# Attention scores computed transposed on halves of the TensorE array's columns, and the read-out's factors multiplied in at its eviction

## The chip, the cores and the metric

The kernel runs on one core of a Trainium2 chip. The metric is device time in microseconds (us); a run's time is that of one execution of the whole program. PE is TensorE, DVE VectorE, ACT ScalarE, POOL GpSimd and SP SyncE, which here only issues transfers.

## The reference

For 8 batches with 8 heads, 512 tokens of width 64 (`x`) and 32 states per head (`state`):

```python
scores = scale * x @ state.T                  # per head: 512 tokens x 32 states
a = softmax(scores, axis=-1)                  # over the 32 states
xread = a @ state                             # 512 x 64
scores2 = scale * state @ x.T                 # the same numbers, transposed: 32 x 512
a2 = softmax(scores2, axis=-1)                # over the 512 tokens
sread = a2 @ x                                # 32 x 64, "the read-out"
rows = concat([xread, sread], axis=2)         # 4608 rows of 512 over all heads
h = rows @ w_in                               # MoE 1, 512 -> 1024
u = layernorm(h * softmax(h)) * g_ln
y = u @ w_out                                 # 1024 -> 512
out = relu(y @ w2_in)**2 @ w2_out             # MoE 2, 512 -> 2048 -> 512
```

Both softmaxes subtract the row's maximum and divide by the sum plus 1e-9.

## The kernel before

**Two phases.** Phase 1 (to about 485 us) does attention and MoE 1 batch by batch, phase 2 MoE 2. The heavy matrix products are done in three passes over operands split into two `fp32r` parts. The attention products between `x` and the states are plain `f32` products; the trace records each of them as two matmul records, and each transpose as one. `xread @ w_in` is folded into `a @ (state @ w_in)`: `emit_sw` makes `sw = state @ w_in` for a batch, `emit_l1` multiplies the transposed softmax `aT` with it.

**Attention of one batch.** Two heads make a pair `hp`, and four heads a group `g` (G = 2); `q` counts the two pairs of a group. `bdf` holds the states as block-diagonal columns with zeros beside them. `scores(b, tp)` (L359) makes scores for half of the tokens: tokens on partitions, the 256 head-state columns along the free axis. ACT copies them to `s_sb` (L367). `softmax_n` takes the softmax over states from `s_sb`: maximum on DVE (L379), subtraction on POOL or DVE (L248), exponential on ACT, sum and reciprocal on DVE (L390 to L392), product on POOL or DVE (L395), result `a_sb`. For the second softmax `emit_sT` (L406) transposes `s_sb` into PSUM (`sTp`), DVE takes the maximum over tokens there (L414), ACT the exponential with the sum as a by-product (L417, `eT`), DVE the reciprocal `l` (L429, L430), and ACT builds `dr`, the identity scaled by `l` (L433). `emit_e` (L447, tile `ep`) multiplies `eT` with `dr`, which transposes back and applies the factor in one f32 product; the copy overwrites `s_sb`. `sread` (L482, tile `srd`) multiplies `x_n` with it, and four small copies put the blocks on the diagonal into `xs`, the rows of the state part.

**The loop.** For batch `b` and `k` of 0 to 7: `emit_lnT` transposes a slice of the normed rows (`lnTp`, evicted to `lt`), `emit_l2` multiplies it with `wo[k]` (the `y` records), and between its four column groups `after[c]` sets pieces of the attention of batch `b+2` and `emit_l1` of batch `b+1`. Scores, `sTp`, `ep`, `aTp`, `srd` and `lnTp` share a pool of two PSUM banks (tag `m`).

**What sets the order.** A planner (`Flow`) runs while the program is built. PE's order is that of the code. Tasks of the other engines are queued with planned costs and due times, and the engine and the place of each instruction come from them: `fl.pe(cost, ...)` advances PE's planned time, a `yield {"V": 0.7}, f, ...` asks for DVE. Each engine then executes its list in that order. At the start SP loads the weights of MoE 1 as 8-byte words, and ACT, DVE and POOL decode them (`decode`: L287, L290, L293, L296, then the split at L242 and L248): eight chunks of `w_in` (`dec_e`, `dec_lt`) and eight of `w_out` (`dec`, then `wo`), which `emit_l2` of batch 0 needs one per `k`.

Of the kernel before, what the change touches and what calls it, by code (L numbers as in the profile page):

```python
# [148 lines left out]
def attn_solu_relu2_kernel(  # L149
# [193 lines left out]
    s_sb, a_sb, aT, sw, u_t, lt, yps, bds = {}, {}, {}, {}, {}, {}, {}, {}  # L343
# [4 lines left out]
    def scores(b, tp):  # L348

        if tp == 0:  # L350
            s_sb[b] = ap_.tile([P, T, HN], F32, tag="s", name="s_sb")
            a_sb[b] = ap_.tile([P, T, HN], F32, tag="a", name="a_sb")
# [16 lines left out]
        done["s", b, tp] = f  # L369
        done["a", b, tp] = fl.spawn(softmax_n(b, tp, f), 8.0 if b else 1.0)  # L370

    def softmax_n(b, tp, f):
        s = s_sb[b][:, 2 * tp:2 * tp + 2, :].rearrange("p t (h n) -> p (t h) n", n=NS)
        a = a_sb[b][:, 2 * tp:2 * tp + 2, :].rearrange("p t (h n) -> p (t h) n", n=NS)
        q = 2 * H
        yield None, 0.0, lambda: f["done"] is not None
        f = f["done"]
        mx = smp.tile([P, q, 1], F32, tag="mx", name="mx")
        f = yield {"V": 0.68}, f, lambda e: nc.vector.tensor_reduce(  # L379
            out=mx, in_=s, axis=AX.X, op=ALU.max  # L380
        )
# [12 lines left out]
        f = yield {"V": 1.2}, f, total
        f = yield {"P": 1.2, "V": 0.69}, f, lambda e: eng_of[e].tensor_tensor(  # L395
            out=a, in0=a, in1=sm.to_broadcast([P, q, NS]), op=ALU.mult
        )
        return f

    def emit_sT(b, g):  # L400


        ps = pm.tile([P, T, P], F32, tag="m", name="sTp")
        fl.pe(0.11 * T, pm_slot(), done["s", b, 0], done["s", b, 1])
        for t in range(T):
            nc.tensor.transpose(ps[:, t, :], s_sb[b][:, t, g * P:(g + 1) * P], ident)  # L406
        pf = ps.rearrange("p t q -> p (t q)")
        et = ap_.tile([P, S], F32, tag="eT", name="eT", bufs=1)
        dr = smp.tile([P, P], F32, tag="dr", name="dr", bufs=1)
        l = smp.tile([P, 1], F32, tag="l2", name="l2", bufs=1)  # L410
        nm = smp.tile([P, 1], F32, tag="m2", name="m2", bufs=1)

        def exps(f):
            f = yield {"V": 0.7}, f, lambda e: nc.vector.tensor_reduce(  # L414
                out=nm, in_=pf, axis=AX.X, op=ALU.max, negate=True
            )
# [5 lines left out]
        first = fl.spawn(exps(fl.end + 0.15), 1.0)  # L422
        pm_free.append(first)

        def rest():
            yield None, 0.0, lambda: first["done"] is not None

            def total(e):
                nc.vector.tensor_scalar(out=l, in0=l, scalar1=1e-9, scalar2=None, op0=ALU.add)  # L429
                nc.vector.reciprocal(out=l, in_=l)  # L430

            f = yield {"V": 0.35}, first["done"], total
            f = yield {"A": 0.4}, f, lambda e: nc.scalar.activation(  # L433
                out=dr, in_=ident, func=AF.Copy, scale=l
            )
            return f

        done["eT", b, g] = et, dr, fl.spawn(rest(), 3.0)

    def emit_e(b, g):  # L440


        et, dr, f = done.pop(("eT", b, g))
        ps = pm.tile([P, T, P], F32, tag="m", name="ep")
        fl.pe(0.23 * T, pm_slot(), f)
        for t in range(T):
            nc.tensor.matmul(  # L447
                out=ps[:, t, :], lhsT=et[:, t * P:(t + 1) * P], rhs=dr, start=True, stop=True
            )

        def gen(f):
            yield None, 0.0, lambda: all(("sub", b, tp) in done for tp in range(T // 2))
            f = yield {"A": 0.6, "V": 0.65}, f, copy(s_sb[b][:, :, g * P:(g + 1) * P], ps)
            return f

        done["e2", b, g] = fl.spawn(gen(fl.end + 0.15), 3.0)
        pm_free.append(done["e2", b, g])

    def emit_aT(b, g):
        f = fl.need([done["a", b, tp] for tp in range(T // 2)])  # L460
# [4 lines left out]
        for t in range(T):  # L465
            nc.tensor.transpose(ps[:, t, :], a_sb[b][:, t, g * P:(g + 1) * P], ident)
# [582 lines left out]
```

## Time and profile before

| | |
|---|---|
| median of 3 runs | 1250.4 us (1249.65 to 1250.83) |
| the profiled execution | 1249.4 us, its span 1247.6 us |
| mean granted clock of TensorE | 0.989 of 2.4 GHz |
| PE busy | 1199.0 us (96%) |
| DVE, ACT, POOL busy | 596.0, 523.8, 206.0 us |

The span runs from the first to the last instruction; 1.8 us of the execution's time lie outside it. A matmul's own duration contains the length of the pipeline, so the time that a run of matmuls takes is read from its start to the start of the next run.

### The profile page before, as it was taken

The numbers are of one execution on the slowest core, as the hardware profiler recorded it, in microseconds if no ns is written. First come the engines' busy times: TensorE is split into PE (matmuls) and PEld (weight loads), VectorE is DVE, ScalarE is ACT, GpSimd is POOL, SyncE is SP. The second block draws the span as 40 slices with busy tenths as digits, with TensorE's granted clock in tenths as the row PEclk, the third lists the DMA queues.
The fourth block names the chain that finished last, engine by engine and source line by source line (L and its number), as shares of the span: only waits on it lengthen the run. The fifth ranks groups of instructions, "written<-read, shape, count | busy, mean of one in ns | idle before, by whom it ended". The sixth has DMA issues, their size and how long they took to land.

```text
span 1247.6 us, 14707 instructions
## 1 busy us (share of the span) xinstructions
PE 1199.0 (96%) x5792; PEld 991.4 (79%) x5792; DVE 596.0 (48%) x940; ACT 523.8 (42%) x937; POOL 206.0 (17%) x243
## 2 busy tenths in 40 slices
PE   5679999999999999979999999999999999999998
PEld 3368888888888887757888888888888888888887
DVE  6975675763854559995322323223223223223232
ACT  4575775765855646544322223223223222222222
POOL 4553133132220423442000000000000000000000
PEclk8899999999999999989999999999999999999999
DMA  7322113112110126541201002002002002010000
GB/s 259 125 82 74 69 40 117 63 46 77 52 58 34 40 86 200 159 152 58 68 1 35 34 1 68 1 1 68 1 1 68 1 1 68 1 51 1 1 34 18
DMA packets 35429, 71.99 MB, mean 58 GB/s; under 512 B 3488, under 2 KB 20896, under 8 KB 34336
## 3 DMA queue, kind: packets, MB, share of 16 engines
q1 hardware_dynamic: 35360, 71.05, 17.2%
q8 instruction: 45, 0.74, 0.2%
q14 instruction: 24, 0.20, 0.1%
HBM read 53.22 MB, written 17.83 MB: 57 GB/s over the span
## 4 chain that ended last, share of the span: by engine, by line
PE 80%; DVE 9%; ACT 5%; DMA 3%; issue 2%; POOL 0%; SPq 0%; ACTq 0%; DVEq 0%
PE o L967 27%; PE h L952 26%; PE y L732 12%; PE hps L662 7%; PE sps L359 2%; PE srd L482 2%; PE lnTp L697 2%; DMA raw<-w_out 2%; DVE dec L290 2%; DVE dec L293 1%; DMA raw<-w_in 1%; ACT e L633 1%; DVE dec L296 1%; PE ep L447 1%; PE hps L513 1%
## 5 line engine op out<-in xcount | busy, mean ns | idle before, releaser
L967 PE MATMUL o<-wb,g 128*128 128x512 f32 x1632 | 398.1, 392 | 9.9 <-DVE g L248 5.4
L952 PE MATMUL h<-yt,wa 128*128 128x512 f32 (+1 forms) x1728 | 394.8, 378 | 0.0
L967 PEld LDWEIGHTS o<-wb,g 128*128 128x128 f32 x1632 | 305.8, 189 | 76.9 <-DVE g L248 8.5
L952 PEld LDWEIGHTS h<-yt,wa 128*128 128x128 f32 x1728 | 314.0, 188 | 61.5
L936 DVE TENSOR_TENSOR r<-r 128x512 f32<-128x512 f32 (+1 forms) x144 | 107.1, 744 | 370.3 <-ACT r L929 370.3
L929 ACT ACTIVATE r<-h 128x512 f32<-128x512 f32 (+1 forms) x144 | 82.5, 573 | 380.5 <-PE h L952 380.5
L732 PE MATMUL y<-lt,wo 128*128 128x512 f32 (+1 forms) x864 | 219.2, 394 | 2.4 <-DVE lt L706 2.0
L732 PEld LDWEIGHTS y<-lt,wo 128*128 128x128 f32 x864 | 150.0, 191 | 28.1 <-DVE lt L706 2.9
L248 DVE TENSOR_TENSOR g<-r,g 128x512 fp32r<-128x512 f32 (+1 forms) x144 | 97.3, 676 | 77.8 <-ACT g L242 71.4
L242 ACT CAST g<-r 128x512 fp32r<-128x512 f32 (+1 forms) x144 | 85.9, 597 | 99.8 <-DVE r L936 98.8
L248 POOL TENSOR_TENSOR yt<-yraw,yt 128x1024 fp32r<-128x1024 f32 (+1 forms) x9 | 20.6, 2288 | 531.6 <-ACT yt L242 531.6
L662 PE MATMUL hps<-sw,aT 128*128 128x512 f32 x368 | 98.2, 415 | 1.8 <-ACT sw L242 1.8
L662 PEld LDWEIGHTS hps<-sw,aT 128*128 128x128 f32 x368 | 69.5, 190 | 23.2 <-issue 6.3
L706 DVE SCALAR_TENSOR_TENSOR lt<-lnTp,g_sb,lt 128x512 fp32r<-128x512 f32 (+1 forms) x72 | 51.5, 716 | 53.9 <-ACT lt L703 53.6
L598 DVE TENSOR_REDUCE hm<-hps 128x1 f32<-128x512 f32 x68 | 46.4, 682 | 47.9 <-PE hps L662 45.8
L242 ACT COPY u<-hps 128x512 f32<-128x512 f32 x68 | 39.7, 584 | 51.5 <-DVE hm L598 49.5
L703 ACT ACTIVATE lt<-lnTp,g_sb 128x512 fp32r<-128x512 f32 (+1 forms) x72 | 48.2, 669 | 11.0 <-PE lnTp L697 10.6
L627 DVE SCALAR_TENSOR_TENSOR u<-u,e 128x1024 f32<-128x1024 f32 x34 | 42.1, 1240 | 13.6 <-ACT e L622 13.6
L633 ACT ACTIVATE e<-u,nmu 128x1024 f32<-128x1024 f32 x34 | 39.1, 1151 | 13.6 <-DVE nmu L630 13.0
L622 ACT ACTIVATE e<-u,nmx 128x1024 f32<-128x1024 f32 x34 | 39.1, 1150 | 12.2 <-issue 7.4
L248 DVE TENSOR_TENSOR sw<-hps,sw 64x512 fp32r<-64x512 f32 (+1 forms) x52 | 35.7, 688 | 14.1 <-ACT sw L242 13.7
L359 PE MATMUL sps<-bdf,xT 128*128 128x128 f32 x256 | 33.5, 288 | 9.2 <-DMA xT<-x_t 6.4
(97 smaller groups left out, 969.7 us busy)
## 6 DMA issues: line engine op xcount, KB each, us to landing
raw<-w_out SPq DMA_DIRECT2D x24, 512.0 KB, 3.5
out<-osb SPq DMA_DIRECT2D x34, 256.0 KB, 2.2
xT<-x_t SPq DMA_DIRECT2D x16, 512.0 KB, 5.3
xn<-x_n SPq DMA_DIRECT2D x8, 1024.0 KB, 4.9
y_d<-ys SPq DMA_DIRECT2D x16, 512.0 KB, 2.6
yraw<-y_d SPq DMA_DIRECT2D x16, 512.0 KB, 5.7
raw<-w_in SPq DMA_DIRECT2D x16, 512.0 KB, 3.8
raw_u<-w_in SPq DMA_DIRECT2D x8, 512.0 KB, 9.1
```

What stands on the lines that cost most here:

```text
L242: nc.scalar.copy(out=out, in_=in_)
L248: return lambda e: eng_of[e].tensor_tensor(out=out, in0=in0, in1=in1, op=ALU.subtract)
L359: nc.tensor.matmul(out=ps[:, j, g * P:(g + 1) * P], lhsT=xT[b][:, 2 * g + (q + b) % 2, (2 * tp + j) * P:(2 * tp + j + 1) * P], rhs=bdf[b][ ...
L633: f = yield {"A": 1.16}, f, lambda e: nc.scalar.activation(out=e_, in_=u, func=AF.Square, bias=nmu, accum_out=vs)
L662: nc.tensor.matmul(out=ps, lhsT=lhsT(i, k), rhs=rhs(j, k)[:, cs], start=(k == 0 and n == 0), stop=(k == n_k - 1 and n == len(passes) - 1),)
L703: f = yield {"A": 0.1 + nt * 0.143}, f, lambda e: nc.scalar.activation(out=o[:, 0], in_=pf, func=AF.Copy, scale=gk)
L706: f = yield {"V": 0.1 + nt * 0.155}, f, lambda e: nc.vector.scalar_tensor_tensor(out=o[:, 1], in0=pf, scalar=gk, in1=o[:, 0].bitcast(F32), ...
L732: nc.tensor.matmul(out=ps, lhsT=wo[k][:, w, c * P:(c + 1) * P], rhs=o[:, a], start=(k == 0 and i == 0), stop=(k == K1 - 1 and i == 2),)
L929: first = one({"A": 0.06 + n / 1000}, lambda e: nc.scalar.activation(out=r, in_=hps, func=AF.Relu))
L936: f = yield {"V": 0.15 + n / 960}, first["done"], lambda e: nc.vector.tensor_tensor(out=r, in0=r, in1=r, op=ALU.mult)
L952: nc.tensor.matmul(out=hps, lhsT=wa[m][:, w, k, :], rhs=yt[j][:, a, k, :], start=(k == 0 and i == 0), stop=(k == KD - 1 and i == 2),)
L967: nc.tensor.matmul(out=ops[j][t], lhsT=g[:, a, t * P:(t + 1) * P], rhs=wb[m][:, w, :], start=(m == 0 and i == 0), stop=(m == K2 - 1 and i ...
```

## The change

**Scores.** `scores(b, g)` now computes the scores of a group of four heads transposed: the states are the stationary operand with 64 columns (`bdf[..., 128 q : 128 q + 64]`), all 512 tokens move, and the product for `q` writes PSUM partitions 64 q to 64 q + 63, which is one half of the array's columns. `s_sb` holds head-states on partitions and tokens along the free axis. `xT` is loaded in halves by head pairs, not by tokens.

**Softmax over tokens.** `max_t` takes the maximum from `s_sb` in SBUF; `exp_t` lets ACT write `eT` with the sum `l2`. There is no `dr`: `emit_e` is four plain transposes. `sread` has 64 columns of `e` as stationary operand and the 128 columns of `x_n` moving, again by halves; its eviction (`sr`, two ACT instructions) multiplies by the reciprocal of `l2`, a factor per partition. `emit_xs` then transposes `sr` back (`xsp`), and the four copies to `xs` read that.

**Softmax over states.** `emit_sT` transposes `s_sb` to tokens on partitions; maximum and subtraction read PSUM, both on DVE; the rest is as before, per group `g`, not per half of the tokens.

**First batch's `sw`.** `emit_sw_first` is written by halves in the same way.

The core of the diff (new `scores`, `exp_t`, parts of `emit_sT`, `sread`, `emit_xs`, and the order):

```diff
-    def scores(b, tp):
...
-        ps = pm.tile([P, 2, HN], F32, tag="m", name="sps")
+    def scores(b, g):
...
+        ps = pm.tile([P, S], F32, tag="m", name="sps")
         slot = pm_slot()
-        for j in range(2):
-            fl.pe(0.87, slot, done["xT", b, tp])
-            for g in range(G):
-                for q in range(2):
-                    nc.tensor.matmul(
-                        out=ps[:, j, g * P:(g + 1) * P],
-                        lhsT=xT[b][:, 2 * g + (q + b) % 2, (2 * tp + j) * P:(2 * tp + j + 1) * P],
-                        rhs=bdf[b][:, g, 64 * q:64 * q + P],
-                        start=(q == 0),
-                        stop=(q == 1),
-                    )
-        s = s_sb[b][:, 2 * tp:2 * tp + 2, :]
+        for q in range(2):
+            fl.pe(0.6, slot, done["xT", b, g])
+            nc.tensor.matmul(
+                out=ps[64 * q:64 * q + 64, :],
+                lhsT=bdf[b][:, g, P * q:P * q + 64],
+                rhs=xT[b][:, 2 * g + (q + b) % 2, :],
+                start=True,
+                stop=True,
+            )
+        s = s_sb[b][:, g, :]
...
+        done["s", b, g] = f
+        done["nm", b, g] = fl.spawn(max_t(b, g, s, f), 6.0)
...
+    def max_t(b, g, s, first):
...
+        f = yield {"V": 0.65}, first["done"], lambda e: nc.vector.tensor_reduce(
+            out=nm, in_=s, axis=AX.X, op=ALU.max, negate=True
...
+        et = e_T[b, g] = ap_.tile([P, S], F32, tag="eT", name="eT", bufs=1)
...
+            yield None, 0.0, lambda: task["done"] is not None
+            f = yield {"A": 0.82}, task["done"], lambda e: nc.scalar.activation(
+                out=et, in_=s, func=AF.Exp, bias=nm, accum_out=l
+            )
...
+    def emit_sT(b, g):
...
+        if g == 0:
+            a_sb[b] = ap_.tile([P, G, T, P], F32, tag="a", name="a_sb")
+        ps = pm.tile([P, T, P], F32, tag="m", name="sTp")
+        fl.pe(0.11 * T, pm_slot(), done["s", b, g])
+        for t in range(T):
+            nc.tensor.transpose(ps[:, t, :], s_sb[b][:, g, t * P:(t + 1) * P], ident)
+        q = T * P // NS
...
+        def subs(f):
             f = yield {"V": 0.7}, f, lambda e: nc.vector.tensor_reduce(
-                out=nm, in_=pf, axis=AX.X, op=ALU.max, negate=True
-            )
-            f = yield {"A": 0.82}, f, lambda e: nc.scalar.activation(
-                out=et, in_=pf, func=AF.Exp, bias=nm, accum_out=l
-            )
+                out=mx, in_=pv, axis=AX.X, op=ALU.max
+            )
+            f = yield {"V": 0.7}, f - fl.HOP, sub(a, pv, mx.to_broadcast([P, q, NS]))
...
+            f = yield {"A": 0.62}, first["done"], lambda e: nc.scalar.activation(
+                out=a, in_=a, func=AF.Exp
...
     def emit_e(b, g):
-        et, dr, f = done.pop(("eT", b, g))
         ps = pm.tile([P, T, P], F32, tag="m", name="ep")
-        fl.pe(0.23 * T, pm_slot(), f)
+        fl.pe(0.11 * T, pm_slot(), done.pop(("eT", b, g)))
+        et = e_T.pop((b, g))
         for t in range(T):
-            nc.tensor.matmul(
-                out=ps[:, t, :], lhsT=et[:, t * P:(t + 1) * P], rhs=dr, start=True, stop=True
-            )
...
+            nc.tensor.transpose(ps[:, t, :], et[:, t * P:(t + 1) * P], ident)
...
     def sread(b):
-        ps = pm.tile([P, HP, P], F32, tag="m", name="srd")
-        e, xb = s_sb.pop(b), xn.pop(b)
...
+        ps = pm.tile([P, G, P], F32, tag="m", name="srd")
+        e, xb, l = s_sb.pop(b).rearrange("p g (t q) -> p g t q", q=P), xn.pop(b), l2[b]
...
-        for hp in range(HP):
-            g = hp // 2
-            fl.pe(0.22 * T, slot, done["xn", b], done["e2", b, g])
+        for g in range(G):
             for t in range(T):
-                nc.tensor.matmul(
-                    out=ps[:, hp, :],
-                    lhsT=xb[:, t, hp * P:(hp + 1) * P],
-                    rhs=e[:, t, g * P:(g + 1) * P],
-                    start=(t == 0),
-                    stop=(t == T - 1),
-                )
+                for q in range(2):
+                    hp = 2 * g + (q + b) % 2
+                    fl.pe(0.16, slot, done["xn", b], done["e2", b, g])
+                    nc.tensor.matmul(
+                        out=ps[64 * q:64 * q + 64, g, :],
+                        lhsT=e[:, g, t, 64 * q:64 * q + 64],
+                        rhs=xb[:, t, hp * P:(hp + 1) * P],
+                        start=(t == 0),
+                        stop=(t == T - 1),
+                    )
+        sr = ap_.tile([P, S], F32, tag="eT", name="sr", bufs=1)[:, :HN].rearrange(
+            "p (g q) -> p g q", g=G
+        )
...
+            f = yield {"V": 0.3}, f, total
+            def scaled(e):
+                for g in range(G):
+                    nc.scalar.activation(
+                        out=sr[:, g, :], in_=ps[:, g, :], func=AF.Copy, scale=l[:, g:g + 1]
...
+            f = yield {"A": 0.6}, f, scaled
...
+    def emit_xs(b):
+        sr, f = done.pop(("sr", b))
+        ps = pm.tile([P, G, P], F32, tag="m", name="xsp")
+        fl.pe(0.22, pm_slot(), f)
+        for g in range(G):
+            nc.tensor.transpose(ps[:, g, :], sr[:, g, :], ident)
...
-                    copy(
-                        xs[rows, hp:HP:2, b * NS:(b + 1) * NS], ps[rows, hp:HP:2, c0:c0 + NS]
-                    )(e)
+                    copy(xs[rows, hp:HP:2, b * NS:(b + 1) * NS], ps[rows, :, c0:c0 + NS])(e)
...
             for q in range(2):
-                fl.pe(0.87, ready, done["bdf", 0], done["w_f", 2 * g + q, c])
+                fl.pe(0.6, ready, done["bdf", 0], done["w_f", 2 * g + q, c])
                 nc.tensor.matmul(
-                    out=ps, lhsT=bdf[0][:, g, 64 * q:64 * q + P], rhs=w_f[2 * g + q, c],
-                    start=(q == 0), stop=(q == 1),
+                    out=ps[64 * q:64 * q + 64, :], lhsT=bdf[0][:, g, P * q:P * q + 64],
+                    rhs=w_f[2 * g + q, c], start=True, stop=True,
...
-    for tp in range(2):
-        scores(0, tp)
+    for g in range(G):
+        scores(0, g)
+    for g in range(G):
+        emit_sT(0, g)
...
     for g in range(G):
         emit_aT(0, g)
+    exp_t(0, 0)```

Each engine's order before and after, at the places where the diff does not tell it. A row is a line, an operation, output<-inputs, the size and how often it repeats; an f32 product is one row entry here and two records in the trace.

PE at the start, from the last `aTp` of batch 0 to its read-out, before:

```order
L466 MATMUL aTp<-ident,a_sb 128x128 x8
L406 MATMUL sTp<-ident,s_sb 128x128 x4
L662 MATMUL hps<-sw,aT 128x512 x2
L447 MATMUL ep<-dr,eT 128x128 x4
L662 MATMUL hps<-sw,aT 128x512 x2
L406 MATMUL sTp<-ident,s_sb 128x128 x4
L662 MATMUL hps<-sw,aT 128x512 x2
L447 MATMUL ep<-dr,eT 128x128 x4
L549 MATMUL hps<-dec_lt,bdf 128x512 x4
L662 MATMUL hps<-sw,aT 128x512 x10
L482 MATMUL srd<-s_sb,xn 128x128 x16
```

PE at the same place, of the change:

```order
L457 MATMUL aTp<-ident,a_sb 128x128 x8
L683 MATMUL hps<-sw,aT 128x512 x2
L444 MATMUL ep<-ident,eT 128x128 x4
L683 MATMUL hps<-sw,aT 128x512 x4
L444 MATMUL ep<-ident,eT 128x128 x4
L570 MATMUL hps<-dec_lt,bdf 64x512 x4
L683 MATMUL hps<-sw,aT 128x512 x10
L476 MATMUL srd<-xn,s_sb 64x128 x16
```

The two `sTp` runs have moved ahead of the first `hps` of the program, and `ep` reads the identity where it read `dr`.

DVE where batch 0 enters the loop, around its first evictions of `lnTp` (`lt`), before:

```order
L414 TENSOR_REDUCE m_611<-sTp 128x1
L248 TENSOR_TENSOR sw<-hps,sw 128x512 x2
L429 TENSOR_SCALAR l_610<-l_610 128x1
L430 RECIPROCAL l_610<-l_610 128x1
L248 TENSOR_TENSOR sw<-hps,sw 128x512
L706 SCALAR_TENSOR_TENSOR lt<-lnTp,g_sb,lt 128x512 x2
L248 TENSOR_TENSOR aT<-aTp,aT 128x512 x2
```

DVE at the same place, of the change:

```order
L248 TENSOR_TENSOR sw<-hps,sw 128x512
L727 SCALAR_TENSOR_TENSOR lt<-lnTp,g_sb,lt 128x512
L248 TENSOR_TENSOR sw<-hps,sw 128x512
L727 SCALAR_TENSOR_TENSOR lt<-lnTp,g_sb,lt 128x512
L290 SCALAR_TENSOR_TENSOR dec<-raw,dec 128x512 x2
L293 TENSOR_SCALAR dec<-dec 128x512
L296 SCALAR_TENSOR_TENSOR dec<-raw,dec 128x512
L293 TENSOR_SCALAR dec<-dec 128x512
L296 SCALAR_TENSOR_TENSOR dec<-raw,dec 128x512
L248 TENSOR_TENSOR aT<-aTp,aT 128x512
L290 SCALAR_TENSOR_TENSOR dec<-raw,dec 128x512
```

Three of the eight decodes of `w_out` (two shown whole, the third by its first instruction) stand behind the first `lt`; before, all eight stand ahead of it.

## Rows read from the trace of the kernel before

**Rows 1.** The page: busy time, share of the span, instructions of each engine.
```profile
PE 1199.0 (96%) x5792; PEld 991.4 (79%) x5792; DVE 596.0 (48%) x940; ACT 523.8 (42%) x937; POOL 206.0 (17%) x243
```

**Rows 2.** Windows: length, busy us (instructions) by engine, granted clock, DMA share, GB/s.
```profile
25.00:57.00 32.00, 21.57 (x63) 11.37 (x62) 31.05 (x42) 18.07 (x34) 18.00 (x12) 0.84 0.32 104
57.00:85.00 28.00, 21.60 (x126) 16.55 (x125) 23.78 (x48) 21.21 (x43) 17.25 (x23) 1.00 0.33 112
85.00:450.00 365.00, 362.60 (x2009) 307.12 (x2007) 214.02 (x401) 230.22 (x429) 91.03 (x152) 1.00 0.18 61
```

**Rows 3.** Waits of PE, whole span: us in total, times, longest.
```profile
PE ep L447 <- ACT dr L433: 13.0, 8, 5.5
```

**Rows 4.** Waits of PE, 85 to 450 us.
```profile
PE ep L447 <- ACT dr L433: 2.0, 4, 0.5
```

**Rows 5.** Timeline of PE, turn of one batch: start us, us, what, records.
```profile
199.64 1.95 PE L359 MATMUL sps<-bdf,xT 128*128 128x128 f32 x16
201.34 1.63 PE L732 MATMUL y<-lt,wo 128*128 128x512 f32 x6
...
222.93 1.05 PE L447 MATMUL ep<-dr,eT 128*128 128x128 f32 x8
223.82 0.60 PE L406 MATMUL sTp<-ident,s_sb 128*128 128x128 f32 x4
224.17 0.93 PE L732 MATMUL y<-lt,wo 128*128 128x512 f32 x3
...
242.00 3.73 PE L482 MATMUL srd<-s_sb,xn 128*128 128x128 f32 x32
245.57 0.60 PE L697 MATMUL lnTp<-ident,u 128*128 128x128 f32 x4
```

**Rows 6.** Timeline of all engines, 30 to 57 us.
```profile
35.44 0.40 ACT L433 ACTIVATE dr<-ident,l 128x128 f32<-128x128 f32 x1
...
35.90 2.08 PE L447 MATMUL ep<-dr,eT 128*128 128x128 f32 x8 [5.47 <-ACT dr L433]
...
47.04 1.16 PE L447 MATMUL ep<-dr,eT 128*128 128x128 f32 x8 [3.10 <-ACT dr L433]
...
48.03 3.60 PE L549 MATMUL hps<-dec_lt,bdf 128*128 128x512 f32 x8
...
51.47 2.74 PE L662 MATMUL hps<-sw,aT 128*128 128x512 f32 x6
```

**Rows 7.** Lines by form: busy us, mean ns of one, idle before.
```profile
L290 DVE SCALAR_TENSOR_TENSOR dec<-raw,dec 128x512 f32<-128x512 f32 x40 | 39.0, 986 | 4.5 <-ACT dec L287 4.5
L296 DVE SCALAR_TENSOR_TENSOR dec<-raw,dec 128x512 int32<-128x512 int32 x40 | 33.8, 846 | 1.0
...
L293 DVE TENSOR_SCALAR dec<-dec 128x512 int32<-128x512 int32 x40 | 31.2, 781 | 0.6
L482 PE MATMUL srd<-s_sb,xn 128*128 128x128 f32 x256 | 29.9, 275 | 0.0
L482 PEld LDWEIGHTS srd<-s_sb,xn 128*128 128x128 f32 x256 | 29.8, 192 | 1.1 <-issue 0.5
...
L248 POOL TENSOR_TENSOR a_sb<-s_sb,mx 128x512 f32<-128x512 f32 x14 | 15.2, 1086 | 130.0 <-DVE mx L379 130.0
...
L242 ACT COPY xs<-srd 64x64 f32<-64x64 f32 x32 | 6.6, 206 | 18.6 <-PE srd L482 18.3
...
L248 DVE TENSOR_TENSOR a_sb<-s_sb,mx 128x512 f32<-128x512 f32 x2 | 1.4, 685 | 0.0
```

**Rows 8.** Timeline of PE, 58 to 86 us.
```profile
70.46 2.05 PE L359 MATMUL sps<-bdf,xT 128*128 128x128 f32 x16 [2.80 <-ACT xs L242]
...
77.71 1.16 PE L447 MATMUL ep<-dr,eT 128*128 128x128 f32 x8 [0.54 <-ACT dr L433]
...
83.97 1.16 PE L447 MATMUL ep<-dr,eT 128*128 128x128 f32 x8 [1.90 <-ACT dr L433]
84.96 0.60 PE L697 MATMUL lnTp<-ident,u 128*128 128x128 f32 x4
```

More of the change, by code (lines that the diff above doesn't have):

```diff
@@ new lines, in emit_sT @@
+    def emit_sT(b, g):
+        if g == 0:
+            a_sb[b] = ap_.tile([P, G, T, P], F32, tag="a", name="a_sb")
[4 more added lines that the diff above has]
+        q = T * P // NS
+        a = a_sb[b][:, g].rearrange("p t (h n) -> p (t h) n", n=NS)
+        pv = ps.rearrange("p t (h n) -> p (t h) n", n=NS)
+        mx = smp.tile([P, q, 1], F32, tag="mx", name="mx")
+        sm = smp.tile([P, q, 1], F32, tag="sm", name="sm")
+        def subs(f):
+            f = yield {"V": 0.7}, f, lambda e: nc.vector.tensor_reduce(
+                out=mx, in_=pv, axis=AX.X, op=ALU.max
+            )
+            f = yield {"V": 0.7}, f - fl.HOP, sub(a, pv, mx.to_broadcast([P, q, NS]))
+            return f
+        first = fl.spawn(subs(fl.end + 0.15), 1.0)
@@ L426, in rest @@
             yield None, 0.0, lambda: first["done"] is not None
+            f = yield {"A": 0.62}, first["done"], lambda e: nc.scalar.activation(
+                out=a, in_=a, func=AF.Exp
+            )
             def total(e):
[L429 to L434, printed above, removed]
+                nc.vector.tensor_reduce(out=sm, in_=a, axis=AX.X, op=ALU.add)
+                nc.vector.tensor_scalar(out=sm, in0=sm, scalar1=1e-9, scalar2=None, op0=ALU.add)
+                nc.vector.reciprocal(out=sm, in_=sm)
+            f = yield {"V": 1.2}, f, total
+            f = yield {"P": 1.2, "V": 0.69}, f, lambda e: eng_of[e].tensor_tensor(
+                out=a, in0=a, in1=sm.to_broadcast([P, q, NS]), op=ALU.mult
             )
             return f
-        done["eT", b, g] = et, dr, fl.spawn(rest(), 3.0)
+        done["a", b, g] = fl.spawn(rest(), 8.0 if b else 1.0)
     def emit_e(b, g):
-        et, dr, f = done.pop(("eT", b, g))
         ps = pm.tile([P, T, P], F32, tag="m", name="ep")
-        fl.pe(0.23 * T, pm_slot(), f)
+        fl.pe(0.11 * T, pm_slot(), done.pop(("eT", b, g)))
+        et = e_T.pop((b, g))
         for t in range(T):
-            nc.tensor.matmul(
-                out=ps[:, t, :], lhsT=et[:, t * P:(t + 1) * P], rhs=dr, start=True, stop=True
-            )
[L451 to L456, printed above, removed]
+            nc.tensor.transpose(ps[:, t, :], et[:, t * P:(t + 1) * P], ident)
+        done["e2", b, g] = one(
+            {"A": 0.6, "V": 0.65}, copy(s_sb[b][:, g, :], ps.rearrange("p t q -> p (t q)"))
+        )
         pm_free.append(done["e2", b, g])
     def emit_aT(b, g):
-        f = fl.need([done["a", b, tp] for tp in range(T // 2)])
+        f = fl.need(done["a", b, g])
         if g == 0:
@@ L818, in attn_solu_relu2_kernel @@
     nc.sync.dma_start(out=g_sb, in_=g_ln.rearrange("(k p) -> p k", p=P))
-    for tp in range(2):
-        scores(0, tp)
+    for g in range(G):
+        scores(0, g)
+    for g in range(G):
+        emit_sT(0, g)
     emit_sw_first(0)
@@ L835, in attn_solu_relu2_kernel @@
     load_xn(1)
-    for tp in range(2):
-        scores(1, tp)
+    for g in range(G):
+        scores(1, g)
+    emit_xs(0)
     for c in range(C1):
         emit_sT(1, c)
+        exp_t(1, c)
         run(emit_sw_alone(1, c, True))
@@ L866, in attn_solu_relu2_kernel @@
                 after[1].append(lambda: sread(b + 1))
+                after[3].append(lambda: emit_xs(b + 1))
                 if nn:
@@ L889, in attn_solu_relu2_kernel @@
                 emit_sw_at(2, HP - 1, k, after)
+            if b >= 1 and nxt and k == 0:
+                after[3].append(lambda: emit_xs(b + 1))
             if b == B - 2 and k == 7:
```

78 lines of the change are left out of this document (30 added, 48 removed).

## The prediction

> **What bounds the kernel now.** I read the page's first part first: PE is busy for 1199.0 of 1247.6 us, 96%, and no other engine reaches half [rows 1]. An average over stages says little, so windows come next [rows 2]. From 85 to 450 us, the loop over the batches, PE is busy for 362.6 of 365.0 us at a granted clock of 1.00 (2.4 GHz): there a microsecond of PE work removed is a microsecond won. Between 25 and 57 us it is otherwise: DVE is busy for 31.05 of 32.00, PE for 21.57, at a mean clock of 0.84; from 57 to 85 no engine is full (ACT 21.21 and DVE 23.78 of 28) and the chain of the first batch sets the end. The list of waits says on what PE lost its time there: 13.0 us on `ep` waiting for the diagonal `dr` that ACT makes [rows 3], of which only 2.0 fall into the loop [rows 4]. Phase 2 is not touched.
>
> **The loop: PE's work per batch.** The timeline gives cadences (start of one run to start of the next), which is what counts, since a record's own duration contains its pipeline [rows 5].
>
> *ep.* Eight records take 222.93 to 223.82, 0.89 us: four f32 products in two records each. Four transposes (`sTp`) take 223.82 to 224.17, 0.35 us. The change makes `ep` such transposes: −0.54 twice per batch, −1.08.
>
> *Scores.* Sixteen records of 128 columns take 199.64 to 201.34, 1.70 us (0.106 each), two runs per batch: 3.40. Afterwards a batch has four products with 512 moving columns, eight records. An f32 record of 512 columns has a cadence of 0.43 (eight of `L549` from 48.03 to 51.47) [rows 6]: 3.44 one after the other, so without overlap nothing is won. The two products of a pair lie on different halves of the array's columns. No record of before uses less than 128x128, so the trace cannot show whether halves run side by side. Bounds: 1.72 if they always do, 3.44 if never. In program order the pair's records are 1a, 1b, 2a, 2b, and only 1b and 2a are neighbours on different halves, which gives three slots of four: 2 x 3 x 0.43 = 2.58. I take that, near the middle of the bounds: −0.82.
>
> *Read-out.* 32 records take 242.00 to 245.57, 3.57 us [rows 5]. Afterwards there are 32 again, with 64 weight columns. Alone: 32 x 0.106 = 3.4. In a long alternating run every border between products can pair, 17 slots, 1.8. Short records have less to hide a weight load behind: a load lasts 192 ns [rows 7] against a cadence of 0.11. So I take 24 slots, 2.55: −1.02. New are two transposes of `xsp`, half of 0.35: +0.18.
>
> *Borders.* Each batch has three runs in halves, six borders. Entering or leaving the form may cost the pipeline's tail: 275 ns for one record [rows 7] less a cadence of 0.106 is 0.17, so 0 to 1.0 per batch. I take 0.5, the middle, since no row has such a border. The Trainium skill ("TensorEngine Tiling (Array Packing)", Key Properties) says that a change of tiling mode drains the engine, which would be the upper bound, 1.0. By it the loop would win 3 us less; no run of before can show it.
>
> Sum per batch: −1.08 − 0.82 − 1.02 + 0.18 + 0.5 = −2.24. Batches 2 to 7 run wholly in the loop: −13.4. Batch 1's read-out lies in it too: −1.02 + 0.18 + two borders at 0.08 = −0.7. Of the 2.0 us of waits for `dr` in the loop [rows 4] I take half, −1.0 (bounds 0 and −2.0): the maximum is now made from SBUF early and `dr` is gone, but `ep` still waits for ACT's exponential. Loop: −15.1.
>
> *Costs I set at nothing there.* The subtraction moves from POOL (14 of 16, 1086 ns) to DVE (685 ns) [rows 7], since POOL's old operand is now in PSUM: 12 x 0.69 = 8.3 us more on DVE, which has 214.0 of 365.0 busy; it hides in the idle 41%. If it were exposed it would cost up to 8.3 us, through the `lt` evictions queued behind it. ACT trades 16 `dr` for 16 scaled evictions. PSUM's two `m` banks take one turn more per batch (`xsp`), three `y` groups or so after `srd`.
>
> **The start, up to 85 us.** PE waits there for `dr` four times: 5.47 at 35.90 and 3.10 at 47.04 [rows 6], 0.54 at 77.71 and 1.90 at 83.97 [rows 8], together 11.0. Less work comes on top: four `ep` −2.2, the second `sw` run, eight records as in the scores (3.44 to 2.58), −0.86, batch 0's read-out −0.84, batch 1's scores −0.82: −4.7. So PE alone would give up to −15.7. But DVE is full until 57 us, so what is late next is DVE. The order shows its change up to the first `lt` (84.96 is where `lnTp` starts): three decodes of `wo` fewer, each 0.986 + 0.781 + 0.846 = 2.61 us as measured in their surroundings [rows 7], −7.8; two subtractions more, +1.4; the four copies of `xs`, by ACT's row 0.206 each, +0.8; three pairs of `l` leave, counted at nothing. Net −5.6. The decodes are not gone but done in the loop, where DVE has room. Against it: the first batch's subtractions and maxima stand ahead of its decodes, so its first `aTp` comes about 2 us later, and 2.80 us of waiting for a PSUM bank at 70.46 [rows 8] stays in another shape (the bank is freed by two scaled evictions). Bounds 0 and −14. I take −8: beyond DVE's 5.6, because PE also falls idle long enough here for the clock to sink (0.84), and far from −14, because DVE is 97% busy.
>
> **Sum.** −15.1 − 8 = −23.1: span 1247.6 to 1224.5. The profiled execution was 1249.4, 1.8 above its span, and the median 1250.4, so 1227.
>
> **The rivals.**
> *Full overlap.* Scores 1.72, read-out 1.8, borders nothing: −1.08 − 1.68 − 1.77 + 0.18 = −4.35, times six −26.1; batch 1's read-out −1.6; waits −2; start −10. Total −39.7: 1211. For it: records of half the columns have nothing in common but the rows. Against: both records of one product need the same half.
> *No overlap.* Scores +0.04, read-out −0.17, −0.53 per batch: −3.2; batch 1 +0.2; waits −1; start −6.5. Total −10.5: 1240.
> *The start gives nothing*, because the extra DVE work of batch 0 delays `aTp` and the chain behind it as much as the decodes free: −15.1, 1235.
> *Slower: weight loads lie open.* If loads for one half cannot run under records of the other, each half-form record pays a load, half of 0.192: 40 x 0.096 = +3.84 on top of no overlap, +3.3 per batch, +19.9; batch 1's read-out +3.3; start −2.5; waits −1. Total +19.7: 1270. It decides for slower from about 30 ns per record (10.5 us over some 340 records). The trace speaks against it: today's read-out has loads of 192 ns and records at a cadence of 0.11, so a load does run under its neighbour's record on the same rows [rows 5, 7]. The Trainium skill ("TensorE: Matmul & The Clock Gate", Part 3, The mechanism) says that a load overlaps records in flight only where the row group differs, and column halves share theirs; by that rule it would be this rival, and the rows of full-array loads disagree with it.
>
> **How the numbers follow.** Chances: forecast 0.47, no overlap 0.18, full overlap 0.15, nothing at the start 0.10, open loads 0.07, and 0.03 for an unlisted wait that eats it all. All but the last two are faster. A measurement of this kernel tells 0.2% (2.5 us) from no change; a mix of no overlap and nothing at the start could end within it. Faster 0.86, same 0.04, slower 0.10. The range 1209 to 1245 holds the four faster cases with their bounds and leaves out the slow ones.
>
> **What would show it.** Each step has its rows: `ep` four records in 0.35; a score pair in 1.29 (0.87 full, 1.72 none); `srd` near 2.55 (1.8 or 3.4); at a run's ends a gap of up to 0.17; PE's waits for `dr` gone and none of their size for `eT`; `lnTp` of batch 0 starting near 77 instead of 84.96; DVE near 65% in the loop with PE still full. It is wrong if a score pair takes over 1.8, or if PE shows waits for `sr`, `xs` or `a_sb` of more than some microseconds.

## The result and the profile after

The changed kernel takes 1218.21 us (median of 4 runs, 1217.06 to 1220.39) against 1250.62 for the kernel before on the same chip: a ratio of 0.9744, with an interval of 0.9727 to 0.976. That is 32.4 us, against 23 forecast; the time lies in the stated range (1209 to 1245).

The page's first part of the changed kernel, which answers to [rows 1]:

```profile
PE 1174.0 (96%) x5552; PEld 943.0 (78%) x5552; DVE 595.9 (49%) x938; ACT 521.8 (43%) x933; POOL 206.0 (17%) x233
```

PE is busy 25.0 us less and its share is the same 96%. Windows of the changed kernel, columns as in [rows 2]:

```profile
25.00:57.00 32.00, 23.73 (x94) 11.57 (x96) 30.18 (x50) 21.49 (x43) 19.16 (x16) 0.82 0.39 139
57.00:85.00 28.00, 24.08 (x125) 17.37 (x122) 23.58 (x45) 19.03 (x38) 14.70 (x20) 0.83 0.26 80
85.00:450.00 365.00, 362.36 (x1930) 288.05 (x1928) 237.18 (x427) 245.10 (x458) 106.14 (x154) 1.00 0.21 73
```

In the loop PE stays full (362.36 of 365.00) while DVE rises from 214.0 to 237.2 us, partly because a loop that ends earlier brings decodes of MoE 2's weights into the window (13.8 us on DVE, from 428 us on; the three deferred decodes of `w_out` are done by 85 us). The span splits at two marks on PE, the first `y` record (the loop's start) and the first `h` record (phase 2). I measure the kernels at these marks:

| | first `y` | loop, first `y` to first `h` | span |
|---|---|---|---|
| before | 86.39 | 400.13 | 1247.6 |
| changed | 72.19 | 381.24 | 1216.7 |
| difference | −14.2 | −18.9 | −30.9 |

The missing +2.2 lies in phase 2, whose code is untouched; over the eleven further kernels below this stretch varies by about as much. PE's timeline of the changed kernel in the turn of one batch, which answers to [rows 5]:

```profile
181.58 1.08 PE L357 MATMUL sps<-xT,bdf 128*64 128x512 f32 x4
182.59 1.66 PE L753 MATMUL y<-lt,wo 128*128 128x512 f32 x6
...
204.63 0.60 PE L444 MATMUL ep<-ident,eT 128*128 128x128 f32 x4
204.98 0.94 PE L753 MATMUL y<-lt,wo 128*128 128x512 f32 x3
...
221.30 1.97 PE L476 MATMUL srd<-xn,s_sb 128*64 128x128 f32 x32
223.20 0.66 PE L718 MATMUL lnTp<-ident,u 128*128 128x128 f32 x4
...
226.50 0.38 PE L511 MATMUL xsp<-ident,sr 128*128 128x128 f32 x2
226.64 3.02 PE L683 MATMUL hps<-sw,aT 128*128 128x512 f32 x12
```

A pair of score products takes 1.01 us from start to next start, where sixteen records took 1.70; the read-out 1.90 (3.57); `ep` 0.35 here (0.89), 0.43 where `sTp` follows it; `xsp` is new. The records' form is 128*64, and four records of 512 columns fit into little more than two of 0.43. PE's timeline at the start:

```profile
28.78 3.59 PE L683 MATMUL hps<-sw,aT 128*128 128x512 f32 x4
32.19 0.62 PE L444 MATMUL ep<-ident,eT 128*128 128x128 f32 x4
32.64 3.60 PE L683 MATMUL hps<-sw,aT 128*128 128x512 f32 x8
36.08 0.60 PE L444 MATMUL ep<-ident,eT 128*128 128x128 f32 x4
36.61 1.94 PE L570 MATMUL hps<-dec_lt,bdf 128*64 128x512 f32 x8
...
47.26 1.97 PE L476 MATMUL srd<-xn,s_sb 128*64 128x128 f32 x32
...
56.67 1.98 PE L357 MATMUL sps<-xT,bdf 128*64 128x512 f32 x4 [6.51 <-ACT sr L496]
...
68.31 0.49 PE L718 MATMUL lnTp<-ident,u 128*128 128x128 f32 x3
71.08 0.77 PE L718 MATMUL lnTp<-ident,u 128*128 128x128 f32 x5 [2.29 <-DVE u L672]
72.19 0.73 PE L753 MATMUL y<-lt,wo 128*128 128x512 f32 x2 [0.34 <-ACT lt L724]
```

Neither `ep` of batch 0 waits any more (5.47 and 3.10 us before, [rows 6]). PE's waits of the changed kernel, over the whole span (total, times, longest):

```profile
PE sps L357 <- ACT sr L496: 6.5, 1, 6.5
...
PE aTp L457 <- POOL a_sb L430: 4.3, 2, 3.6
...
PE y L753 <- DVE lt L727: 3.0, 3, 1.2
PE lnTp L718 <- DVE u L672: 2.3, 1, 2.3
```

`dr` has left the list. New are 6.5 us for `sr`, at 56.67, 4.3 us of `aTp` for `a_sb`, and 2.3 us for the last normed `u`.

To see where the loop's 18.9 us come from, I add up, for each tile, the times from a record's start to the next PE record's start, between the two marks. A wait therefore stands with the record ahead of it, not with the one that waits:

| tile | before | changed | difference | forecast |
|---|---|---|---|---|
| `sps` | 20.41 | 12.11 | −8.3 | −4.9 |
| `srd` (7 read-outs) | 24.91 | 13.28 | −11.6 | −7.1 |
| `ep` | 11.03 | 5.62 | −5.4 | −6.5 |
| `xsp` | 0 | 1.24 | +1.2 | +1.3 |
| all others (`y` +2.7, `aTp` +0.9, `hps` +0.9, `lnTp` +0.6, `sTp` +0.1) | | | +5.2 | +2.2 (borders +3.2, waits for `dr` −1.0) |

### The profile page after: what moved, and what is told of

The parts are those of the page before. It is cut to its first block, busy times and chain, and to the rows that moved or that the text cites. A ratio compares the mean times of both kernels' runs of the same rounds, so it can differ in the third digit from the quotient of the medians.

```text
span 1216.7 us, 14244 instructions
## 1 busy us (share of the span) xinstructions
PE 1174.0 (96%) x5552; PEld 943.0 (78%) x5552; DVE 595.9 (49%) x938; ACT 521.8 (43%) x933; POOL 206.0 (17%) x233
## 4 chain that ended last, share of the span: by engine, by line
PE 84%; DVE 8%; DMA 4%; ACT 2%; issue 1%; SPq 0%; ACTq 0%; DVEq 0%
PE o L999 28%; PE h L984 27%; PE y L753 14%; PE hps L683 7%; PE lnTp L718 2%; DMA raw<-w_in 2%; DMA raw<-w_out 2%; PE hps L534 1%; DVE dec L290 1%; PE sps L357 1%; DVE dec L293 1%; PE srd L476 1%; DVE dec L296 1%; DMA raw_u<-w_in 1%; DVE r L968 1%
## 5 line engine op out<-in xcount | busy, mean ns | idle before, releaser
L968 DVE TENSOR_TENSOR r<-r 128x512 f32<-128x512 f32 (+1 forms) x144 | 110.7, 768 | 367.4 <-ACT r L961 367.4
L753 PE MATMUL y<-lt,wo 128*128 128x512 f32 (+1 forms) x864 | 222.3, 397 | 3.8 <-DVE lt L727 3.0
L753 PEld LDWEIGHTS y<-lt,wo 128*128 128x128 f32 x864 | 150.6, 192 | 40.8 <-issue 9.9
L248 DVE TENSOR_TENSOR g<-r,g 128x512 fp32r<-128x512 f32 (+1 forms) x144 | 97.5, 677 | 78.2 <-ACT g L242 72.8
L242 ACT CAST g<-r 128x512 fp32r<-128x512 f32 (+1 forms) x144 | 85.7, 595 | 102.6 <-DVE r L968 102.0
L248 POOL TENSOR_TENSOR yt<-yraw,yt 128x1024 fp32r<-128x1024 f32 (+1 forms) x9 | 20.5, 2287 | 533.6 <-ACT yt L242 448.8
L683 PE MATMUL hps<-sw,aT 128*128 128x512 f32 x368 | 98.5, 417 | 0.0
L683 PEld LDWEIGHTS hps<-sw,aT 128*128 128x128 f32 x368 | 69.0, 190 | 21.5 <-issue 6.4
L727 DVE SCALAR_TENSOR_TENSOR lt<-lnTp,g_sb,lt 128x512 fp32r<-128x512 f32 (+1 forms) x72 | 51.7, 717 | 37.3 <-ACT lt L724 37.1
L242 ACT COPY u<-hps 128x512 f32<-128x512 f32 x68 | 39.5, 582 | 48.3 <-DVE hm L619 47.2
L662 POOL TENSOR_SCALAR es<-es 128x1 f32<-128x1 f32 x34 | 32.5, 957 | 158.4 <-ACT e L643 157.4
L724 ACT ACTIVATE lt<-lnTp,g_sb 128x512 fp32r<-128x512 f32 (+1 forms) x72 | 48.1, 669 | 11.4 <-PE lnTp L718 11.1
L718 PE MATMUL lnTp<-ident,u 128*128 128x128 f32 x272 | 42.2, 275 | 2.7 <-DVE u L672 2.3
```

The source lines that it names most:

```text
L242: nc.scalar.copy(out=out, in_=in_)
L248: return lambda e: eng_of[e].tensor_tensor(out=out, in0=in0, in1=in1, op=ALU.subtract)
L683: nc.tensor.matmul(out=ps, lhsT=lhsT(i, k), rhs=rhs(j, k)[:, cs], start=(k == 0 and n == 0), stop=(k == n_k - 1 and n == len(passes) - 1),)
L718: nc.tensor.transpose(ps[:, t, :], u_t[key, t][:, k * P:(k + 1) * P], ident)
L724: f = yield {"A": 0.1 + nt * 0.143}, f, lambda e: nc.scalar.activation(out=o[:, 0], in_=pf, func=AF.Copy, scale=gk)
L727: f = yield {"V": 0.1 + nt * 0.155}, f, lambda e: nc.vector.scalar_tensor_tensor(out=o[:, 1], in0=pf, scalar=gk, in1=o[:, 0].bitcast(F32), ...
```

## The experiments

**The read-out with one half after the other.** Do halves overlap because neighbours lie on different halves, or is a record of 64 columns simply twice as fast?

```diff
-        for g in range(G):
-            for t in range(T):
-                for q in range(2):
+        for q in range(2):
+            for g in range(G):
+                for t in range(T):
```

> The changed kernel with the read-out's products in another order: all of the first half of the columns, then all of the second, so that neighbours lie on the same half. Theory O (two halves overlap, neighbours must lie on different halves): a read-out goes from 1.90 us to about 3.5 (32 records at 0.109), +1.6 each, seven of them in the loop: +11 to +13 us in all. Rival F (a record of 64 columns simply runs at twice the rate, whatever its neighbour): 1.9 as now, +0 to 1.

Measured: 1227.21 us, 9.0 more than the changed kernel; seven read-outs in the loop take 22.81 in place of 13.28. That is a little under the 11 to 13 expected. PE's timeline, one read-out and what follows:

```profile
225.65 3.33 PE L476 MATMUL srd<-xn,s_sb 128*64 128x128 f32 x32
228.91 0.66 PE L718 MATMUL lnTp<-ident,u 128*128 128x128 f32 x4
```

Thirty-two records take 3.26 us, 102 ns each and about what the old form had. The form alone is worth little; F falls, and the gain is overlap.

**How far apart may the partners be?** The same products alternating by twos and by fours:

```diff
-            for t in range(T):
-                for q in range(2):
+            for t, q in ((0, 0), (1, 0), (0, 1), (1, 1), (2, 0), (3, 0), (2, 1), (3, 1)):
+                for _ in range(1):
```

```diff
-            for t in range(T):
-                for q in range(2):
+            for q in range(2):
+                for t in range(T):
```

> The changed kernel with the read-out's products alternating by twos between the halves (two on the first, two on the second), not one by one. One by one the records start in pairs 6 ns apart, two per 0.109 us. If PE starts a record ahead of older ones that wait for the other half, and looks at least four records ahead, a read-out stays at 1.9 us (59 ns per record). If only neighbours overlap, three of eight records find a partner at the borders: 0.08 to 0.1 per record, 2.6 to 3.0 us.

> The same with four products on one half, then four on the other. With a look ahead of eight records or more it stays at 1.9 us; with four it lies between the order by twos and the order with a whole half at a time (102 ns per record, 3.26 us); with neighbours alone 0.095 to 0.1.

Measured, one profiled run each: 1217.06 and 1220.53 us. A read-out by twos:

```profile
221.59 2.02 PE L476 MATMUL srd<-xn,s_sb 128*64 128x128 f32 x32
223.54 0.66 PE L718 MATMUL lnTp<-ident,u 128*128 128x128 f32 x4
```

and by fours:

```profile
223.02 2.57 PE L476 MATMUL srd<-xn,s_sb 128*64 128x128 f32 x32
225.52 0.66 PE L718 MATMUL lnTp<-ident,u 128*128 128x128 f32 x4
```

By twos it is 1.95, as good as one by one; by fours 2.50 (78 ns per record); a half at a time 3.26. So partners need not be neighbours: with two products (four records) of one half ahead of two of the other the overlap is still whole. The starts of the single records show the reach: where four products or a whole half stand together, the last four records of one half go in pairs with the first four of the next half, and the others follow alone, 0.109 us apart. By fours 24 of the 32 records find a partner, a half at a time 8. Whether PE itself takes later records first or the build already interleaves the two records of a product, these traces don't tell; either way the step "in program order only 1b and 2a are neighbours" was wrong.

**Scores over the whole array,** transposed as in the change, but zero-padded:

```diff
-                out=ps[64 * q:64 * q + 64, :],
-                lhsT=bdf[b][:, g, P * q:P * q + 64],
+                out=ps,
+                lhsT=bdf[b][:, g, 64 * q:64 * q + P],
...
-                start=True,
-                stop=True,
+                start=(q == 0),
+                stop=(q == 1),
```

> The changed kernel with the transposed scores as two zero-padded products over the whole array (four records of 512 columns at 0.43, 1.74 us) in place of a pair on halves (1.01, and 0.13 at its two borders). Theory O: +0.6 per run, 12 in the loop, +7 to +9 us in all, and the 0.1 us by which the y run ahead of each score run is longer now goes away. Rival (borders and new waits have eaten what the halves win): under +3.

Measured: 1224.57 us, +6.4; the loop +5.1. PE's timeline:

```profile
184.27 1.88 PE L357 MATMUL sps<-xT,bdf 128*128 128x512 f32 x4
185.59 1.97 PE L753 MATMUL y<-lt,wo 128*128 128x512 f32 x6
```

Four records take 1.32 to the next start, and the `y` record behind them starts while the last still streams (the `y` sum grows by 2.7 us). The halves of the scores are worth about 6 us, a little under the 7 expected. Without them the transposed scores cost about what the 16 small records did; the rest of the change is still worth 25 us in this run (1249.83 for the kernel before on its chip).

**`ep` as an f32 product.**

```diff
-            nc.tensor.transpose(ps[:, t, :], et[:, t * P:(t + 1) * P], ident)
+            nc.tensor.matmul(
+                out=ps[:, t, :], lhsT=et[:, t * P:(t + 1) * P], rhs=ident, start=True, stop=True
+            )
```

> The changed kernel with ep made as an f32 product with the identity again, not as a transpose; nothing else moves. If ep's term is what it was priced at, eight records take 0.89 us in place of 0.35 to 0.44: +0.5 each, 12 in the full loop and some of the 4 at the start, +5.5 to +8 us. Rival: the gain booked under ep came from the waits that went with dr, then under +3.

Measured: 1223.31 us, +5.1, just under the lower end. `ep` costs 4.6 us more in the loop (10.19 against 5.62), 0.38 each, and the first `y` comes 3.6 later; phase 2 was 1.8 shorter in this trace. PE's timeline:

```profile
210.22 1.05 PE L444 MATMUL ep<-ident,eT 128*128 128x128 f32 x8
211.03 0.94 PE L755 MATMUL y<-lt,wo 128*128 128x512 f32 x3
```

Eight records take 0.81 ahead of `y`, where four transposes take 0.35. The loop's gain under `ep` is in the records, not in the waits.

**The decodes of `w_out` due early again.**

```diff
+    fl.mark([done["wo", k] for k in range(K1)], fl.end - 12.0)
     emit_lnT(0, 0, T)
```

> The changed kernel with all eight decodes of w_out made due before the loop, as they were before the change (five are ahead of the first lt now). If the deferred decodes carry half of the start's 14 us (theory D), the first y starts 5 to 8 us later, at 77 to 80 us, and the time rises by as much. Rival W (the start was won where PE waited for dr, DVE's queue is not what ends it): first y within 2 us of 72.2 and the time within 3.

Measured: 1228.0 us, +9.8. The first `y` starts at 78.14, 5.9 later: theory D holds for the start. The loop is 4.5 us longer too, which no theory had. PE's waits in it (78 to 470 us):

```profile
PE y L753 <- DVE lt L727: 3.8, 4, 1.4
PE sTp L401 <- ACT s_sb L242: 3.7, 5, 0.7
```

The planner laid out ACT and DVE otherwise, and PE waits for evictions. I count only the 5.9 as the decodes' price. Of it, 2.65 us are a wait of the second `sTp` for DVE's `a_sb` (L248), and 1.6 are the twelve `hps` records behind it, which take 4.43 us (2.82 in the changed kernel), at a granted clock of 1.2 GHz for most of that time.

**The kernel before with one `sTp` moved.**

```diff
+    emit_sT(0, 0)
     emit_sw_first(0)
...
-        (emit_e if i % 2 else emit_sT)(0, i // 2)
+        if i:
+            (emit_e if i % 2 else emit_sT)(0, i // 2)
```

> The kernel before with one thing moved: the first sTp of batch 0 stands ahead of its first sw products, so that the maximum, the exponential and dr are done long before ep asks for dr at 35.9. No halves, no transposes. Theory W (the start's gain is the waits for dr): the wait of 5.5 us goes, the first y starts 5 to 8 us earlier than 86.4, and the time falls by as much. Rival D (DVE's queue is full to 57 us, so the wait only moves behind it): first y within 2 us of 86.4.

Measured: 1242.78 us, a ratio of 0.9948 (0.9934 to 0.9961), with all eight decodes still ahead of the loop. First `y` at 79.67, 6.7 earlier; the loop is unchanged (400.07). PE's timeline:

```profile
30.03 1.05 PE L447 MATMUL ep<-dr,eT 128*128 128x128 f32 x8
...
39.16 1.16 PE L447 MATMUL ep<-dr,eT 128*128 128x128 f32 x8 [4.20 <-ACT dr L433]
```

The first `ep` waits no longer, the second waits 4.2 in place of 3.1. W holds as well: four transposes moved, with no halves at all, give 6.7 us at the start.

**The subtraction twice.**

```diff
             f = yield {"V": 0.7}, f - fl.HOP, sub(a, pv, mx.to_broadcast([P, q, NS]))
+            f = yield {"V": 0.7}, f - fl.HOP, sub(a, pv, mx.to_broadcast([P, q, NS]))
```

> The changed kernel with the subtraction after the maximum, which moved from POOL to DVE, done twice: 16 x 0.69 us more on DVE. If DVE has room for it in the loop, as was counted, the 12 there cost nothing and the 4 at the start at most 2.8 us: +0 to 3. Rival (the move is exposed and eats part of the gain): +8 to 11.

Measured: 1218.36 us (1215.75 to 1221.5), +0.15. The window of the loop, columns as in [rows 2]:

```profile
85.00:450.00 365.00, 361.55 (x1918) 284.81 (x1916) 244.62 (x441) 245.63 (x458) 108.80 (x158) 1.00 0.21 73
```

DVE is busy 7.4 us more there and the loop takes 381.95, 0.7 more: in the loop the subtraction is hidden, as it was counted. At the start it is not shown to be free: in this trace, the slowest of its four runs, the first `y` comes at 74.98, 2.8 later, as much as the four there were expected to cost at most.

**PE's wait for `sr` filled.**

```diff
-    for g in range(G):
-        scores(1, g)
+    scores(1, 0)
+    run(emit_sw_alone(1, 0, True))
+    scores(1, 1)
     emit_xs(0)
-    for c in range(C1):
-        emit_sT(1, c)
-        exp_t(1, c)
-        run(emit_sw_alone(1, c, True))
-        emit_e(1, c)
+    emit_sT(1, 0)
+    exp_t(1, 0)
+    run(emit_sw_alone(1, 1, True))
+    emit_e(1, 0)
+    emit_sT(1, 1)
+    exp_t(1, 1)
     emit_lnT(0, 0, T)
+    emit_e(1, 1)
```

> The changed kernel with the first half of batch 1's sw products put between the two score runs of batch 1, where PE now waits 6.5 us at 56.67 for the eviction sr to free a bank. If that wait ends on the path that sets the loop's start, the first y comes 3 us earlier (the 12 records moved into it) and the time falls by 2 to 4 us. Rival: the normed rows u, ready at 71.0, set the loop's start (lnTp waits 2.3 us for DVE there), and the wait costs nothing: within 1 us of now.

Measured: 1219.51 us, +1.3, first `y` at 74.90, 2.7 later and not 3 earlier. PE's waits up to 90 us:

```profile
PE lnTp L718 <- DVE u L672: 3.6, 1, 3.6
PE sps L357 <- ACT sr L496: 3.4, 1, 3.4
```

The wait for `sr` halved, and `lnTp` waits longer for `u` (3.6, before 2.3). The 6.5 us were covered by another chain.

**Five decodes held back,** in place of three:

```diff
+    gate = []
+
+    def gated(k):
+        yield None, 0.0, lambda: k < 3 or bool(gate)
+        f = yield from decode(wo[k][:, 0], wo[k][:, 1], w_out[k * P:(k + 1) * P, :])
+        return f
+
...
-        done["wo", k] = fl.spawn(decode(wo[k][:, 0], wo[k][:, 1], w_out[k * P:(k + 1) * P, :]), 20.0)
+        done["wo", k] = fl.spawn(gated(k), 20.0)
...
     emit_lnT(0, 0, T)
+    gate.append(True)
```

> The changed kernel with the last five decodes of w_out held back until batch 0's first lnTp is set (three ahead of the first lt, where the change has five). Theory D: two decodes fewer at 2.6 us on DVE bring the first y 3 to 5 us forward from 72.2, and the time to 1213 to 1216, if the five fit into batch 0's loop. Rival: from here ACT's exponentials set the start, not DVE, and the first y stays within 1.5 us of 72.2. Second rival: wo comes late for its k, and y waits for POOL or DVE by some us, so the time rises.

Measured: 1214.51 us (1213.69 to 1216.42), a ratio of 0.9717 (0.9704 to 0.9731) to the kernel before, 3.7 us under the changed kernel and with no run as slow as its fastest. PE's timeline:

```profile
55.70 1.98 PE L357 MATMUL sps<-xT,bdf 128*64 128x512 f32 x4 [5.63 <-ACT sr L496]
...
67.76 0.60 PE L718 MATMUL lnTp<-ident,u 128*128 128x128 f32 x4
68.65 0.66 PE L718 MATMUL lnTp<-ident,u 128*128 128x128 f32 x4 [0.29 <-ACT s_sb L242]
69.24 0.73 PE L753 MATMUL y<-lt,wo 128*128 128x512 f32 x2
```

The first `y` starts at 69.24, 2.95 earlier, the wait for `u` is gone, and the loop (380.54) takes the five decodes without a loss. This is the fastest version of the study.

**Both edits together,** the held decodes and the filled wait:

> The last two edits together: the last five decodes of w_out held back, and the first half of batch 1's sw products put into PE's wait for sr. With the decodes held back the last normed u of batch 0 is ready at 64.4 us and lnTp waits only 0.3 us more, so PE's own order sets the start now, and its wait of 5.6 us at 55.7 should no longer be free: the 3 us of products moved into it bring the first y from 69.2 to 66 to 67, and the time to 1211 to 1213. Rival (that wait is covered by another even now): first y within 1 us of 69.2, time as with the held decodes alone, 1214.5.

Measured: 1219.31 us, slower than the held decodes alone. The first `y` is where it was, 69.26:

```profile
50.34 3.04 PE L591 MATMUL hps<-wi,bdr 128*128 128x512 f32 x12
55.74 1.24 PE L357 MATMUL sps<-xT,bdf 128*64 128x512 f32 x4 [2.36 <-ACT sr L496]
...
58.71 1.09 PE L401 MATMUL sTp<-ident,s_sb 128*128 128x128 f32 x4 [1.11 <-DVE xs L244]
...
65.52 0.52 PE L718 MATMUL lnTp<-ident,u 128*128 128x128 f32 x3 [0.39 <-ACT s_sb L242]
66.55 0.33 PE L718 MATMUL lnTp<-ident,u 128*128 128x128 f32 x1 [0.51 <-POOL u L672]
66.74 0.63 PE L444 MATMUL ep<-ident,eT 128*128 128x128 f32 x4
68.85 0.66 PE L718 MATMUL lnTp<-ident,u 128*128 128x128 f32 x4 [1.48 <-ACT s_sb L242]
69.26 0.71 PE L753 MATMUL y<-lt,wo 128*128 128x512 f32 x2
```

The 12 records did move into the wait for `sr`, but the time comes back as waits for `xs`, for PSUM banks (`s_sb`) and for `u`; the loop is 4.5 us longer, with waits for `lt` (4.5 us, 2.6 with the held decodes alone) among them. My expectation fell; the rival was right on the first `y`, not on the time. The order of the other engines' lists changed too, so these causes were not separated.

## Why the prediction held, and where it was off

**Direction and bound: right.** PE is full in the loop, and what PE lost in work came off the time. The cost set at nothing on DVE holds in the loop: the doubled subtraction adds 0.7 us there. Two of the signs that were to show the forecast wrong did appear, PE's waits for `sr` (6.5) and for `a_sb` (4.3). The first turned out to cost nothing; the second was not tested.

**Overlap of the halves: right in kind, too small.** The forecast took three slots of four for a score pair (1.29) and 24 slots of 32 for the read-out (2.55). Measured are 1.01 and 1.90. The step that failed is the order argument: partners need not be neighbours, they reach across four records. Inside a read-out two records go per 0.109 us, the cadence of one full-array record, so the overlap is whole, and what lies above the full-overlap bounds of 0.87 and 1.8 stands at the ends of the run (next paragraph). This term was −4.9 − 7.1 and came out as −8.3 − 11.6. Without the 2.9 us of borders in it, it is −22.8, where the rival of full overlap, at a chance of 0.15, had −22.5. On this step that rival was right; the stated range was wide enough to hold both.

**Borders: more than I took.** I took 0.08 each, 0.17 for a run, with 0.34 as the bound. Measured from the starts of the single records: the record ahead of a run in halves takes 0.32 to 0.33 us to the next start where it takes 0.23 ahead of other work, 0.09 more. The first pair in a run takes 0.05 more than one record of the same length, the last pair 0.10 more. The first record behind the run takes 0.02 (a `y` behind scores) to 0.06 (an `lnTp` behind a read-out) more. Together that is 0.27 for a score run and 0.30 for a read-out, some 5.2 us for the 19 runs in the loop against 3.2 forecast; 2.3 of it stand in the rows of other tiles, 2.9 in `sps` and `srd`. My middle was too low; the Trainium skill's rule on draining ("TensorEngine Tiling (Array Packing)", Key Properties), which stood for the upper bound, came nearer.

**Open weight loads: did not happen.** Groups by form of the changed kernel (busy us, mean ns of one, idle before):

```profile
L476 PEld LDWEIGHTS srd<-xn,s_sb 128*64 128x64 f32 x256 | 13.8, 137 | 3.3 <-issue 1.1 <-DVE aT L248 1.1 <-DVE lt L727 1.1
...
L248 DVE TENSOR_TENSOR a_sb<-sTp,mx 128x512 f32<-128x512 f32 x16 | 10.9, 687 | 0.4
...
L357 PEld LDWEIGHTS sps<-xT,bdf 128*64 128x64 f32 x64 | 3.5, 148 | 20.3 <-ACT sr L496 7.4 <-issue 6.4 <-ACT u L242 3.7
```

Loads of 64 columns last 137 ns, and 32 of them go by in a read-out of 1.90 us; one after the other and outside the records they alone would need 4.4. They run under records of the same rows, which by the Trainium skill's rule on row groups ("TensorE: Matmul & The Clock Gate", Part 3, The mechanism) they would not; here the trace disagrees with it.

**`ep`: about right.** −5.4 where −6.5 was forecast. 0.7 of the difference is one wait of an `sTp` for a PSUM bank, which the table counts with the `ep` ahead of it. The forecast also compared an `ep` ahead of `sTp` (0.89) with an `sTp` ahead of `y` (0.35); ahead of `sTp` the new `ep` takes 0.43. The waits for `dr` in the loop, 2.0 us [rows 4], are gone whole, where I took half; in the table they stood with `y`.

**The rest of the loop: +5.2 where +2.2 stood.** Borders are 2.3 of it. The waits in these rows fell by 0.7: the 2.0 for `dr` are gone, those for `lt` and `aT` grew by less. About 1.4 is the clock: from 73.2 to 76.6 us, just behind the first `y`, it is granted at 1.2 GHz, and four `aTp` ahead of `y` take 0.71 us there and 0.35 in the later batches. (One more such stretch near the loop's end, at 438.4 to 441.8 us and at 472.2 to 475.6 before, costs the same in both kernels.) The remaining 2 us are the `y` records named below.

**The start: −14.2 where −8 stood.** The failed step is that I set one bound against the other: DVE's own saving (−5.6) against PE's (−15.7), and stayed near DVE's, because DVE is 97% busy. With all eight decodes put back ahead of the loop, the changed kernel still starts it at 78.14, 8.2 us earlier than before; deferring three of them gives 5.9 more. What bound PE was less the length of DVE's list than the place in it of the chain that PE waits for: the kernel before, with the same eight decodes, gains 6.7 us when one `sTp` is moved. That DVE was full said that its total mattered, not that order did not. How the 8.2 divides between order and less work in the changed kernel was not separated. The other reason for going beyond DVE's 5.6, the clock, did not come true: from 25 to 57 us the mean granted clock is 0.82 (0.84 before), from 57 to 85 it is 0.83 (1.00 before), and ahead of the first `y` 23.9 us run at 1.2 GHz against 17.1. The start became shorter although the clock was lower.

**What stays open:** `y` records are 2 to 3 ns longer in every version with the change (median 233 against 231 ns inside a `y` run), also in the last two batches, which have no attention beside them. It is some 2 us; no experiment was aimed at it.

## What to carry to other kernels

Products with 64 stationary columns overlap in pairs when their outputs lie on different halves, and the order must bring both halves within about two products (four records) of each other; set a whole half ahead of the other and little is left of it (3.26 us for a read-out, 1.90 one by one, 3.57 in the old form). A run in halves also pays at its ends, here 0.27 to 0.30 us, so short runs gain less. Where PE waits on a chain through a full engine, look at the place of that chain in the engine's list before counting the list's length, and hold back what is needed only later. A wait in the list of waits is worth its length only while no other chain ends later: the 6.5 us for `sr` were worth nothing.

## What was not expected of the hardware

The first records of the two halves start 6 ns apart one by one and 13 ns apart by twos, though the products are issued one after the other on the same engine; by fours they still overlap in part (78 ns per record, against 59 and 102).
